# A's key weights on two DMA queues: rows 2, 4 and 6 issued by ScalarE, each after a one-column copy

## The chip, the cores and the metric

The kernel runs on one core of a Trainium2 chip. The time is the device time of one execution in microseconds; before the change the median of five runs is 474.25 us (474.18 to 474.83).

A core has TensorE (PE, matrix products), VectorE (DVE), ScalarE (ACT), GpSimd (POOL) and SyncE (SP). In a profile "PEld" is the loading of the stationary operand of a matmul, and "SPq" or "ACTq" is an engine at issuing a DMA.

## The reference, cut to what matters

Two attention blocks read the same `x` (2048 rows of 1024, bf16) and are mixed by a gate. Block A is linear attention; its keys are where the change lies.

```python
x = A_x
g = _sigmoid((x * gate_w).sum(-1, keepdims=True))
a = _A_ref(x, A_wqkv, A_wo)      # linear attention, 32 heads of 32
b = _B_ref(x, B_wqkv, B_wo)      # dilated sliding window, 8 keys
return g * a + (1 - g) * b

# in _A_ref
phi = lambda t: jnp.where(t > 0, t + 1, jnp.exp(t)) + 1e-6
pq, pk = phi(q), phi(k)          # q, k, v = x @ wqkv, split
kv = jnp.einsum("bhsd,bhse->bhde", pk, v)
z = jnp.einsum("bhsd->bhd", pk)
o = num / den                    # pq with kv, pq with z
return o ... @ wo
```

## The kernel before, in words

The contraction over the 1024 inputs is cut into KT = 8 pieces of 128 rows, numbered by `kt`; the 2048 tokens are cut into NB = 16 blocks of 128, numbered by `t`. The stages follow each other on TensorE: A's keys `pk` (line 167), the product of `x` with `pk` (line 218), A's key-value matrix (238), B's values and A's queries (293 and 329), B's keys, queries and attention (387, 444, 466), and the output (584).

The change lies in the loads that feed the first stage. `WkA` (128 x 8 x 1024) holds the key columns of `A_wqkv`; "row kt" of it is 128 partitions by 1024, 256 KB, loaded by `load_wk` (line 99) on the queue of the engine that is given to it. `xT` holds `x` transposed; `load_xT` (line 95) loads its columns `kt` for the first four blocks by a DMA transpose from SyncE, and line 112 the other twelve blocks, 128 tokens each with all eight `kt`. Behind them on SyncE come the rows of `x`, the gate's weights and further weights (lines 113 to 121).

The order on SyncE and ScalarE is written out by hand (`manual_schedule`), and so is the order on TensorE. ScalarE issues row 0, SyncE issues everything else: `xT` 0, row 1, `xT` 1, row 2, `xT` 2-3, row 3, row 4, `xT` 4-5, row 5, row 6, `xT` 6-7, row 7, and then line 112. DMAs share eight completion semaphores in rotation; one that takes up a semaphore again waits until the earlier transfer on it has landed.

TensorE first runs 37 products of ones (`warm_up`, line 173). Then it takes the first four blocks and both halves of the 1024 columns together, in eight PSUM banks, and goes through the contraction in groups, so that it can start with the first rows:

```python
for kts_ in ((0,), (1,), (2, 3), (4, 5), (6, 7)):
    for half in range(2):
        for t in range(4):
            for kt in kts_:
                project(first[4 * half + t], t, kt, half)
```

Thus 8 products use row 0, 8 use row 1, and then 16 in turns rows 2 and 3. When the last group is through, `phi` (lines 153 to 155, ScalarE and VectorE) turns each bank into `pk`; after that block after block follows. `ones` is a constant tile, there before the first instruction of the program's body. ScalarE's first instruction is the load of a function table (line 68); after its issue of row 0 its next work is the first exponential of line 153.

Of the kernel before, what the change touches and what calls it, by code (L numbers as in the profile page):

```python
# [39 lines left out]
def kernel(  # L40
# [11 lines left out]
    nc = tc.nc  # L52
# [6 lines left out]
    def rows(ap, s0, s1):  # L59
        return ap[s0 // 1024, s0 % 1024:(s1 - 1) % 1024 + 1, :]  # L60
# [3 lines left out]
    KT = D // P  # L64
# [12 lines left out]
    def load_w(name, src, col0, tag, only=(0, 1)):  # L77
        halves = []
        for h in only:
            w = wpool.tile([P, KT, 512], BF16, name=f"{name}{h}", tag=tag)  # L80
            c0 = col0 + h * 512
            nc.sync.dma_start(out=w[:], in_=src[:, c0:c0 + 512].rearrange("(kt p) n -> p kt n", p=P))
            halves.append(w)
        return halves
# [4 lines left out]
    def load_rows(eng, t0, t1):  # L89
        eng.dma_start(out=xrow[:, t0:t1, :], in_=rows(x, t0 * P, t1 * P).rearrange("(t p) d -> p t d", p=P))  # L90

    WkA = wide.tile([P, KT, D], BF16, name="WkA", tag="wa")

    def load_xT(kt, n, t0, t1):
        nc.sync.dma_start_transpose(out=xT[:, kt:kt + n, t0 * P:t1 * P],  # L95
                                    in_=rows(x, t0 * P, t1 * P)[:, kt * P:(kt + n) * P])

    def load_wk(eng, kt):
        eng.dma_start(out=WkA[:, kt, :], in_=A_wqkv[kt * P:(kt + 1) * P, D:2 * D])  # L99

    ones = nc.const_aps.tensor(1.0, [P, P], BF16)
    with tc.manual_schedule(engines={SP, mybir.EngineType.Activation}):
        load_wk(nc.scalar, 0)
        load_xT(0, 1, 0, 4)
        load_wk(nc.sync, 1)
        load_xT(1, 1, 0, 4)
        for kt in range(2, KT):
            load_wk(nc.sync, kt)
            if kt % 2 == 0:
                load_xT(kt, 2, 0, 4)  # L110
        for t in range(4, NB):
            nc.sync.dma_start_transpose(out=xT[:, :, t * P:(t + 1) * P], in_=rows(x, t * P, (t + 1) * P))
        for t in range(0, NB, 4):
            load_rows(nc.sync, t, t + 4)
        gw_row = consts.tile([P, D], BF16, name="gw_row")
        nc.sync.dma_start(out=gw_row[:], in_=gate_w.partition_broadcast(P))
        WvA = load_w("WvA", A_wqkv, 2 * D, "wb")
        WoA = load_w("WoA", A_wo, 0, "wo")
        WvB = load_w("WvB", B_wqkv, 2 * D, "wc")
# [37 lines left out]
    with tc.manual_schedule(engines={PE}):  # L157

        with ExitStack() as s1:
# [42 lines left out]
            for t in range(1, NB):  # L202
                side.append(lambda t=t: nc.vector.tensor_tensor(
                    out=zacc[:], in0=zacc[:] if t > 1 else pk[:, 0, :], in1=pk[:, t, :], op=ALU.add))
            side.append(lambda: nc.gpsimd.partition_all_reduce(zrow[:], zacc[:], P, bass_isa.ReduceOp.add))
            for t in range(NB):
                side.append(lambda t=t: nc.vector.tensor_tensor_reduce(
                    out=gjunk[:], in0=xrow[:, t, :], in1=gw_row[:], scale=1.0, scalar=0.0, op0=ALU.mult,
# [151 lines left out]
        with ExitStack() as s2:  # L360
# [158 lines left out]
            for c in range(KT):  # L519
                kts[c] = kpool.tile([P, 2, 1024], BF16, name="kt", tag="kt")  # L520
                for hh in range(2):
# [3 lines left out]
                    if 1 <= c <= 2:  # L525
                        t = 2 * (c - 1) + hh
                        nc.sync.dma_start_transpose(out=pqT[0][:, :, t * P:(t + 1) * P],
                                                    in_=pqd[t * P:(t + 1) * P, :])
# [114 lines left out]
```

The softmax here doesn't subtract the row's maximum and nothing guards it: scores larger than these inputs give would overflow.

## Time and profile before

| | |
|---|---|
| median of five runs | 474.25 us (474.18 to 474.83) |
| the profiled execution's own time | 474.25 us |
| its span, first to last instruction | 472.5 us |
| PE busy | 468.5 us (99%) |
| DVE, ACT, POOL busy | 277.3, 169.1, 15.3 us |
| DMA moved | 55.40 MB, 117 GB/s on the mean |
| granted TensorE clock | 1.000 |
| ScalarE, first exponential of line 153 | starts at 17.14 us, after 15.06 us idle |
| SyncE, line 112 | first issued at 11.50 us, twelve in 17.35 us |

The busy time of an engine is the sum of its instructions; matmuls overlap, so a busy PE may still be slower than its peak. The "chain of waits" follows the program back from its last instruction to whatever released each step. A line of the timeline gives the start, the length, the engine, the source line, the operation, and in brackets the idle time before it with what ended it. In a table of stretches each row gives the stretch, its length, then busy time and count for PE, PEld, DVE, ACT and POOL, the granted clock, the share of the DMA engines (above 1 where packets overlap) and GB/s.

### The profile page before, as it was taken

What the parts mean: (1) busy time and instruction counts of PE and PEld (TensorE: products, weight loads), DVE (VectorE), ACT (ScalarE), POOL (GpSimd) and SP (SyncE); (2) the same over time, 40 slices, a digit from 0 to 9 for tenths busy, and PEclk for the clock granted to TensorE, in tenths of its full rate; (3) what the DMA queues carried; (4) which work ended last, traced back from release to release, by engine and by line L of the source; (5) the groups of instructions that cost most, each with busy time, mean ns of one, the idle gap of its engine ahead of it and who ended that gap; (6) DMA issues with size and microseconds to landing.
All of it is one profiled execution on the core that took longest, in us unless ns stands there. A gap on an engine that the chain in (4) does not pass through costs nothing.

```text
span 472.5 us, 13171 instructions
## 1 busy us (share of the span) xinstructions
PE 468.5 (99%) x5765; PEld 246.3 (52%) x5765; DVE 277.3 (59%) x601; ACT 169.1 (36%) x272; POOL 15.3 (3%) x30
## 2 busy tenths in 40 slices
PE   9999999999999999999999999999999999999997
PEld 5444444445444444445666666666665444444444
DVE  0496689990329999999567676767660049800000
ACT  1343321102533333333555555555551134221122
POOL 3300000500000000000000000000000000000000
PEclk9999999999999999999999999999999999999999
DMA  8999960000644233627326626442563843221101
GB/s 199 225 255 371 348 227 0 0 1 0 203 129 120 95 139 130 156 95 246 108 55 102 112 52 94 100 95 50 92 151 79 177 123 78 69 54 45 34 33 46
DMA packets 96716, 55.40 MB, mean 117 GB/s; under 512 B 70162, under 2 KB 86546, under 8 KB 96658
## 3 DMA queue, kind: packets, MB, share of 16 engines
q1 hardware_dynamic: 91618, 50.10, 41.4%
q10 hardware_dynamic: 5040, 4.46, 2.9%
q8 instruction: 45, 0.74, 0.6%
q14 instruction: 13, 0.11, 0.1%
HBM read 26.10 MB, written 15.86 MB: 89 GB/s over the span
## 4 chain that ended last, share of the span: by engine, by line
PE 97%; SPq 1%; DMA 1%; issue 0%; ACT 0%
PE q_ps L387 27%; PE d_ps L584 12%; PE p_ps L293 12%; PE g_ps L218 12%; PE e_ps L584 12%; PE pk_ps L167 11%; PE p_ps L329 9%; PE po L466 2%; PE s2b L444 2%; DMA WkA<-in_A_wqkv_dram 1%; SPq L95 1%; PE kv_ps L238 0%; PE w_ps L281 0%; SPq L99 0%; ACT osb L589 0%
## 5 line engine op out<-in xcount | busy, mean ns | idle before, releaser
L387 PE MATMUL q_ps<-xT,WqB 64*64 64x512 bf16 x1024 | 68.3, 377 | 0.0
L387 PE MATMUL q_ps<-xT,WkB 64*64 64x512 bf16 x1024 | 67.9, 377 | 0.0
L154 DVE TENSOR_SCALAR e<-e 128x512 f32<-128x512 f32 x64 | 27.0, 422 | 64.5 <-ACT e L153 64.5
L293 PE MATMUL p_ps<-WvB,xT 128*128 128x512 bf16 x256 | 57.7, 379 | 0.0
L167 PE MATMUL pk_ps<-WkA,xT 128*128 128x512 bf16 x256 | 56.5, 383 | 0.3 <-DMA WkA<-in_A_wqkv_dram 0.3
L218 PE MATMUL g_ps<-pk,xrow 128*128 128x512 bf16 x256 | 55.4, 379 | 0.0
L449 ACT ACTIVATE PT<-s2b 128x928 bf16<-128x928 f32 (+4 forms) x40 | 34.2, 854 | 45.5 <-PE s2b L444 45.5
L451 DVE TENSOR_TENSOR PT<-PT,mask 128x928 bf16<-128x928 bf16 (+4 forms) x40 | 23.6, 590 | 38.1 <-ACT PT L449 38.1
L329 PE MATMUL p_ps<-WqA,xT 128*128 128x512 bf16 x192 | 43.4, 379 | 0.0
L584 PEld LDWEIGHTS <-pqT 128*128 128x128 bf16 x272 | 26.0, 98 | 29.8 <-issue 0.4
L167 PEld LDWEIGHTS <-xT 128*128 128x128 bf16 x256 | 25.2, 99 | 31.2 <-issue 1.9
L584 PEld LDWEIGHTS <-OBT 128*128 128x128 bf16 x272 | 26.0, 98 | 29.4
L218 PEld LDWEIGHTS <-xrow 128*128 128x128 bf16 x256 | 25.0, 98 | 30.2
L293 PEld LDWEIGHTS <-xT 128*128 128x128 bf16 x256 | 24.7, 98 | 30.2 <-issue 0.9
L387 PEld LDWEIGHTS <-WkB 64*64 64x64 bf16 x1024 | 31.7, 107 | 15.4 <-issue 0.4
L387 PEld LDWEIGHTS <-WqB 64*64 64x64 bf16 x1024 | 31.4, 106 | 15.4 <-issue 0.7
L153 ACT ACTIVATE e<-pk_ps 128x512 f32<-128x512 f32 x32 | 18.9, 597 | 41.2 <-PE pk_ps L167 37.0
L298 ACT CAST tmp<-p_ps 128x512 bf16<-128x512 f32 x32 | 18.8, 590 | 35.9 <-PE p_ps L293 29.4
L584 PE MATMUL d_ps<-WoA,pqT 128*128 128x512 bf16 (+1 forms) x136 | 30.9, 370 | 0.0
L584 PE MATMUL d_ps<-WoB,OBT 128*128 128x512 bf16 (+1 forms) x136 | 30.8, 370 | 0.0
L329 PEld LDWEIGHTS <-xT 128*128 128x128 bf16 x192 | 18.8, 98 | 22.6
L584 PE MATMUL e_ps<-WoA,pqT 128*128 128x512 bf16 (+2 forms) x136 | 30.0, 363 | 0.0
(61 smaller groups left out, 486.6 us busy)
## 6 DMA issues: line engine op xcount, KB each, us to landing
vd<-tmp SPq DMA_DIRECT2D x16, 264.0 KB
xrow<-in_A_x_dram SPq DMA_DIRECT2D x4, 1024.0 KB
out_dram<-osb ACTq DMA_DIRECT2D x31, 128.0 KB
pqd<-tmp SPq DMA_DIRECT2D x12, 256.0 KB
WvA<-in_A_wqkv_dram SPq DMA_DIRECT2D x2, 1024.0 KB
WoA<-in_A_wo_dram SPq DMA_DIRECT2D x2, 1024.0 KB
WvB<-in_B_wqkv_dram SPq DMA_DIRECT2D x2, 1024.0 KB
WqA<-in_A_wqkv_dram SPq DMA_DIRECT2D x1, 2048.0 KB
```

Of the source, the lines that this page charges most:

```text
L153: nc.scalar.activation(out=e[:], in_=pj[:], func=ACT.Exp)
L154: nc.vector.tensor_scalar(out=e[:], in0=e[:], scalar1=1.0, scalar2=1e-6, op0=ALU.min, op1=ALU.add)
L167: nc.tensor.matmul(pj[:], lhsT=xT[:, kt, t * P:(t + 1) * P], rhs=WkA[:, kt, half * 512:half * 512 + 512], start=(kt == 0), stop=(kt == KT ...
L218: nc.tensor.matmul(pj[:], lhsT=xrow[:, t, kt * P:(kt + 1) * P], rhs=pk[:, t, half * 512:(half + 1) * 512], start=(t == 0), stop=(t == NB - 1))
L293: nc.tensor.matmul(st["pj"][:], lhsT=xT[:, kt, t * P:(t + 1) * P], rhs=WvB[half][:, kt, :], start=(kt == 0), stop=(kt == KT - 1))
L298: nc.scalar.copy(out=v[:, half * 16:(half + 1) * 16, 0:Dh], in_=st["pj"][:].rearrange("p (h e) -> p h e", h=16))
L329: nc.tensor.matmul(st["pj"][:], lhsT=xT[:, kt, t * P:(t + 1) * P], rhs=WqA[:, kt, half * 512:half * 512 + 512], start=(kt == 0), stop=(kt ...
L387: nc.tensor.matmul(banks[o][64 * j:64 * j + 64, :], lhsT=lhsT(r, kt, j), rhs=rhs(r, kt), start=first and kt == 0, stop=kt == KT - 1, skip_ ...
L444: nc.tensor.matmul(s2b[64 * par:64 * par + 64, pair, :, o:o + w], lhsT=kts[c][r, par, k0:k0 + 64], rhs=qz[r, :, par, q0 % 512:q0 % 512 + w ...
L449: nc.scalar.activation(out=pt[:, :, 0:W_], in_=s2b[:].rearrange("p a b s -> p (a b) s")[:, :, 0:W_], func=ACT.Exp, scale=SCALE)
L451: nc.vector.tensor_tensor(out=pt[:, :, 0:W_], in0=pt[:, :, 0:W_], in1=mask[:, None, base:base + W_].broadcast_to([P, 4, W_]), op=ALU.mult)
L584: nc.tensor.matmul(st["ps"][:, 0:n], lhsT=lhsT, rhs=W[c0 // 512][:, c, c0 % 512:c0 % 512 + n], start=(side == 0 and c == 0), stop=(side == ...
```

## The change

Rows 2, 4 and 6 of `WkA` are issued by ScalarE in place of SyncE. Ahead of each stands a copy, on ScalarE, of one column into that very row: the DMA overwrites the column, so it has to wait for the copy. The copy for row 2 reads `ones`, that for row 4 reads row 0 of `WkA`, and that for row 6 reads row 2, so these two wait until the row that they read has landed. SyncE keeps rows 1, 3, 5 and 7 and all transposes: `xT` 0, row 1, `xT` 1, `xT` 2-3, row 3, `xT` 4-5, row 5, `xT` 6-7, row 7, then the twelve blocks (line 114 after the change).

```diff
         load_xT(0, 1, 0, 4)
         load_wk(nc.sync, 1)
         load_xT(1, 1, 0, 4)
-        for kt in range(2, KT):
-            load_wk(nc.sync, kt)
-            if kt % 2 == 0:
-                load_xT(kt, 2, 0, 4)
+        for kt in (2, 4, 6):
+            src = ones if kt == 2 else WkA[:, kt - 4 if kt == 4 else 2, :]
+            nc.scalar.copy(out=WkA[:, kt, 0:1], in_=src[:, 0:1])
+            load_wk(nc.scalar, kt)
+            load_xT(kt, 2, 0, 4)
+            load_wk(nc.sync, kt + 1)
```

## The prediction

> **What bounds the kernel now.** First the page: TensorE is busy in 468.5 of 472.5 us, and the chain of waits gives it 97%. What is not PE is 1% DMA for `WkA` and about 1% for SyncE's issues of lines 95 and 99.
>
> ```profile
> PE 468.5 (99%) x5765; PEld 246.3 (52%) x5765; DVE 277.3 (59%) x601; ACT 169.1 (36%) x272; POOL 15.3 (3%) x30
> PE 97%; SPq 1%; DMA 1%; issue 0%; ACT 0%
> L167 PE MATMUL pk_ps<-WkA,xT 128*128 128x512 bf16 x256 | 56.5, 383 | 0.3 <-DMA WkA<-in_A_wqkv_dram 0.3
> ```
>
> The reader is to see that line 167, the product with A's key weights, has only 0.3 us of idle time before it. A change in the loading order can win what PE loses at the start, and no more. So next the chain over the first 60 us, in order of time (start, us, what):
>
> ```profile
> 3.91 0.58 SPq L99
> 4.49 0.04 issue
> 4.53 1.29 SPq L95
> 5.82 0.04 issue
> 5.87 3.91 DMA WkA<-in_A_wqkv_dram
> 9.78 0.04 issue
> 9.82 50.23 PE pk_ps L167 x232
> ```
>
> The chain goes through SyncE's issues one after the other, to the row of `WkA` issued at 5.87 (row 3), which lands at 9.78; from 9.82 PE runs without a gap. Then the timeline of PE and of its weight loads around that point:
>
> ```profile
> 0.84 4.11 PE L173 MATMUL warm<-const-bfloat16-1.0 128*128 128x128 bf16 x37 [0.84 <-PEq L627]
> 4.74 4.80 PE L167 MATMUL pk_ps<-WkA,xT 128*128 128x512 bf16 x17
> 9.82 2.53 PE L167 MATMUL pk_ps<-WkA,xT 128*128 128x512 bf16 x11 [0.28 <-DMA WkA<-in_A_wqkv_dram]
> 4.63 0.25 PEld L167 LDWEIGHTS <-xT 128*128 128x128 bf16 x2
> 6.79 2.04 PEld L167 LDWEIGHTS <-xT 128*128 128x128 bf16 x10 [0.20 <-issue]
> 9.14 0.13 PEld L167 LDWEIGHTS <-xT 128*128 128x128 bf16 x2 [0.30 <-DMA xT<-in_A_x_dram]
> ```
>
> Two stalls: 0.30 us before the weight load of 9.14 (columns 2 and 3 of `xT`), then 0.28 us before the matmul of 9.82 (row 3). Together 0.58 us. The first product starts at 4.63 because the 37 warm-up matmuls end there: `xT` 0 has landed at 4.22 and row 0 at 3.76 by the trace's completion events, and the change touches neither. The spacing of weight loads is 0.43 us up to about 6.5 us and about 0.216 us after 6.79, so PE turns to full speed there.
>
> **What the Trainium skill says.** "DMA: Bandwidth & Descriptors", section "Issuing engines are not separate DMA queues": transfers of SP and ACT run on the same 16 DMA engines, and a second issuer saves only the sequencer's issue time. The trace does show issue times of 0.58 us (SP) and 0.39 us (ACT) for one row, but also DMA time that is not full (below), which a second ring could fill. The same page, section "Queues, rings and completion order": an engine goes round its rings by packets, so a row on ACT's ring shares time with SP's transposes; the trace has nothing of this, since ACT has one early row only. "TensorE: Matmul & The Clock Gate", Part 1: the window that releases the clock runs free, so the point of full speed moves between runs. One profile cannot confirm that; it has the point near 6.6 us.
>
> **The change part by part.** Sums are against the profiled execution: 474.25 us, span 472.5, 1.75 around it; it equals the median of the five runs.
>
> (1) SyncE loses the issues of rows 2, 4 and 6, three of 0.58 us, 1.7 us in all. Columns 2-3 of `xT` go out at 3.91 in place of 4.53, row 3 at 5.25 in place of 5.87, columns 4-5 at about 5.85 (6.96), row 5 at 7.2 (8.40), columns 6-7 at 7.8 (9.49), row 7 at 9.2 (10.88), the twelve transposes of line 112 from 9.8 (11.50). Each reuses one of eight completion semaphores: row 5 waits for row 1, columns 6-7 for row 0, row 7 for columns 2-3. The first two have landed long before (5.73, 3.76); the last landed at 9.10 in this trace, just ahead of SyncE's arrival. So at worst some tenths, with row 7 needed by PE only at 16.5 (below).
>
> (2) ScalarE gains three copies and three issues. The table load ends at 2.08. A 128x1 copy on ScalarE takes 0.16 us here (`seen`, line 399, from PSUM; the nearest row), an issue 0.39. Row 2: copy at 2.1, issue at 2.3 to 2.7, where SyncE had 3.91. Row 4: its copy reads row 0 (landed 3.76), its issue also waits for the semaphore of `xT` 0 (4.22), so 4.3 to 4.7 in place of 6.4. Row 6: its copy reads row 2; from issue to landing the present rows take 2.9 to 4.2 us, so it is issued between 5.5 and 7.0 in place of 8.93. Behind them on ScalarE stands the first exponential of line 153, at 17.14, after 15.06 us idle: six instructions of 1.7 us in all, and two waits that end by 7, cost nothing. That cover would be gone only if row 2 landed after 16.
>
> (3) The order of the bytes. All is moved as before, but row 4 (and part of row 6) now runs ahead of row 3. From the trace's packet records a row is 128 packets of 2 KB at 84 ns, over 16 engines 0.67 us; a 128x512 piece of `xT` is 512 packets of 256 B at 18 ns, 0.58 us. The DMA share by stretches of 1 us:
>
> ```profile
> 4.00:5.00 1.00, 1.00 (x10) 0.89 (x9) 0.00 (x0) 0.00 (x0) 0.00 (x0) 1.00 0.74 240
> 7.00:8.00 1.00, 1.00 (x6) 0.49 (x5) 0.00 (x0) 0.00 (x0) 0.00 (x0) 1.00 0.74 114
> 8.00:9.00 1.00, 1.00 (x7) 0.39 (x4) 0.00 (x0) 0.00 (x0) 0.00 (x0) 1.00 1.17 306
> 9.00:10.00 1.00, 0.72 (x4) 0.23 (x3) 0.00 (x0) 0.00 (x0) 0.56 (x2) 1.00 1.04 341
> ```
>
> The last two columns are the share and GB/s. 114 GB/s at 7 us against 306 and 341 later: the early transfers are slow (single packets of 0.4 to 1.2 us among them), not short of engines. From 3.5 us, when row 1 starts, to 9.0, when the last packet of row 3 starts, are 5.5 us. The work in it is row 1, `xT` 1, row 2, `xT` 2-3, row 3: 0.67 + 0.58 + 0.67 + 1.15 + 0.67 = 3.74 us. So 1.76 us are lost to slow packets, and two rings can hide them behind each other. After the change 0.67 (row 4) to 1.34 us (rows 4 and 6) are added ahead of row 3. If all lost time is filled, row 3's last packet goes at 3.5 + 3.74 + 0.67 = 7.9, or 8.6 with row 6; landing follows some 0.75 us later (9.78 for 9.0): 8.7 to 9.3. If none is filled, 9.78 + 0.67 to 9.78 + 1.34, so 10.4 to 11.1. With two thirds filled (1.17 us) and all of row 4 with half of row 6 in front (1.0): 9.6. I take that. The fill is a choice between two bounds, no row shows it.
>
> (4) What it is worth. Without a stall PE would reach row 3's first product at 9.82 - 0.58 = 9.24. A landing of 9.6 makes that product start at 9.64, 0.18 us sooner; a landing under 9.2 gives the full 0.58. All that follows stays behind PE: at 0.216 us each, the 15 products left of rows 2 and 3 end at 13.1, where rows 4 and 5 are wanted (they land at 10.75 and 12.46 now, and are issued earlier after the change); rows 6 and 7 at 16.5 (14.83 now); `xT` of block 4 at 20.0 (15.79 now). So nothing is late next, and the shift passes to the end undiminished. Row 1 and `xT` 1 are the one point to watch: wanted at 7.2 (the ninth product), landed at 5.73 and 6.31; sharing with row 2 costs at most 0.67 us, so 6.98, still in time. **Sum:** -0.58 to +1.3, taken as -0.2: 474.25 - 0.2 = about 474.0.
>
> **The rivals.** No change that can be measured means within 0.2%, 0.95 us.
> - *Forecast, a small shift* (81%): 473.4 to 475.1, row 3's landing between 8.7 and 10.6. For it: the idle time at stake is 0.58 us.
> - *The holds do not hold, and row 3 is crowded out* (12%, slower): rows 4 and 6 are released by row 0 and row 2, which land before PE is half way through row 1, so they take up to 1.34 us of the engines just as columns 2-3 and row 3 travel. It decides from a landing of 10.73 (9.78 + 0.95); at the full price 474.25 + 1.3 = 475.6. For it: share over 1 from 8 us on. Against it: 114 GB/s at 7 us, room to fill.
> - *All stalls vanish and PE runs ahead* (7%, faster): if in most executions the full clock comes at 4.6 rather than 6.6, PE would reach row 3 by 4.63 + 17 x 0.216 = 8.3 and now waits to 9.78; a landing of 8.7 would then give 1.1 us: 473.15. Against it: it needs the best landing and the early clock together.
> - *It does nothing*: the engines are shared, the fill just pays for row 4; 474.25, part of the first case.
>
> **How the numbers follow.** Likeliest 474.0. Downward the range takes the full stall with a little of the early clock, 473.4; upward a landing of 10.6, 475.1. Faster by over 0.2% (below 473.3) 0.07, slower (above 475.2) 0.12, between them 0.81.
>
> **What would show it.** Right: ACT issues of `WkA` near 2.3, 4.3 and 5.5 to 7; SyncE's line 114 (112 before) starting near 9.8; stalls before row 3's product under 0.6 us; no gap of PE later. Wrong: a wait of PE for `xT` 1 near 7 us, a wait for row 3 beyond 10.7, ACT held past 16, or any PE gap after 13 us that is not there now.

## The result and the profile after

| | before | after |
|---|---|---|
| median | 474.49 us (473.86 to 476.87, 48 runs) | 476.29 us (474.25 to 478.32, 27 runs) |
| profiled execution, its span | 474.25, 472.5 us | 476.77, 475.1 us |
| ratio after to before | | 1.0031, 95% interval 1.0022 to 1.0040 |

The change makes the kernel slower, by 0.3% or 1.8 us between the medians (1.0 to 1.9 us by the interval); the forecast was 474.0 us in a range of 473.4 to 475.1. A part of the runs of several of these kernels, the one before among them, has a mean TensorE clock of 0.996 in place of 1.000 and is some 2 us longer; where such runs are many (6 of 15 in e2, 8 of 22 in e13, below), the median of the others follows in brackets.

The page of the changed kernel, first PE's row, then the group of line 169 (167 before):

```profile
PE 467.4 (98%) x5765; PEld 244.5 (51%) x5765; DVE 277.3 (58%) x601; ACT 169.7 (36%) x275; POOL 15.4 (3%) x30
L169 PE MATMUL pk_ps<-WkA,xT 128*128 128x512 bf16 x256 | 55.9, 379 | 3.6 <-DMA xT<-in_A_x_dram 3.1
```

PE's idle time before products of this line was 0.3 us and is 3.6 us, and what ended most of it is now a transpose of `xT`, not a row of `WkA`. The chain of waits over the first 60 us (start, us, what):

```profile
3.89 1.30 SPq L95
5.19 0.04 issue
5.24 6.73 DMA WkA<-in_A_wqkv_dram
11.96 0.04 issue
12.01 48.07 PE pk_ps L169 x222
```

Row 3 is issued at 5.24 instead of 5.87, as the change wants, but takes 6.73 us to land instead of 3.91. The timeline of PE, then of the weight loads:

```profile
4.24 1.89 PE L169 MATMUL pk_ps<-WkA,xT 128*128 128x512 bf16 x8
8.38 1.90 PE L169 MATMUL pk_ps<-WkA,xT 128*128 128x512 bf16 x8 [2.25 <-DMA xT<-in_A_x_dram]
11.15 0.39 PE L169 MATMUL pk_ps<-WkA,xT 128*128 128x512 bf16 x1 [0.88 <-DMA xT<-in_A_x_dram]
12.01 10.30 PE L169 MATMUL pk_ps<-WkA,xT 128*128 128x512 bf16 x47 [0.47 <-DMA WkA<-in_A_wqkv_dram]
4.19 1.45 PEld L169 LDWEIGHTS <-xT 128*128 128x128 bf16 x8
```

Three stalls: 2.25 us for `xT` 1, 0.88 for `xT` 2-3, 0.47 for row 3. Row 3's first product starts at 12.01, before it was 9.82: 2.19 us later. A gap of 0.4 us on PE in the attention stage, which the trace of the kernel before doesn't have and for which no cause is known, makes 2.6 with it: the two spans differ by 475.1 - 472.5 = 2.6. The eight weight loads in 1.45 us also show PE at full speed from its first product here; before it was so only after 6.5 us.

ScalarE's timeline:

```profile
2.09 0.19 ACT L109 COPY WkA<-const-bfloat16-1.0 128x1 bf16<-128x1 bf16 x1
2.31 0.34 ACTq L99 DMA_DIRECT2D WkA<-in_A_wqkv_dram  x1
3.71 0.19 ACT L109 COPY WkA<-WkA 128x1 bf16<-128x1 bf16 x1 [1.42 <-DMA WkA<-in_A_wqkv_dram]
4.22 0.33 ACTq L99 DMA_DIRECT2D WkA<-in_A_wqkv_dram  x1
6.94 0.20 ACT L109 COPY WkA<-WkA 128x1 bf16<-128x1 bf16 x1 [3.04 <-DMA WkA<-in_A_wqkv_dram]
8.41 0.34 ACTq L99 DMA_DIRECT2D WkA<-in_A_wqkv_dram  x1
```

Row 4 goes out at 4.22, when `xT` 0 has landed. A ring, in what follows, is the queue of one issuing engine; a packet is one piece of a transfer in the trace's records, 2 KB of a row or 256 B of a transpose. The packets of row 4 start at 6.9 us, after the last of row 2 on ScalarE's ring, and end at 10.8, beside the transposes of columns 2-3 on SyncE's ring. Both are slow: a packet of row 4 takes 191 ns on the mean in place of 84, and the transposes pass 19 to 133 packets in each 0.25 us from 7.0 to 9.75. A transpose that travels alone at its best passes about 280 (282 and 284 in the kernel before from 12.75 to 13.25); but it can be slow alone too, as in the kernel before, where 19 to 58 passed in each 0.25 us from 7.0 to 7.75 with nothing on the other ring. So a slow stretch needs no second ring; the changed kernel's is longer. Its stretches (last two columns: DMA share and GB/s):

```profile
6.00:7.00 1.00, 0.13 (x1) 0.00 (x0) 0.00 (x0) 0.06 (x1) 0.00 (x0) 1.00 1.04 164
7.00:8.00 1.00, 0.00 (x0) 0.00 (x0) 0.00 (x0) 0.13 (x1) 0.00 (x0) 1.00 1.27 171
8.00:9.00 1.00, 0.62 (x3) 0.31 (x4) 0.00 (x0) 0.00 (x0) 0.00 (x0) 1.00 1.05 164
```

171 and 164 GB/s from 7 to 9 us where the kernel before had 114 and 306, with the engines no less occupied. From 6 to 7 us the kernel before had 233:

```profile
6.00:7.00 1.00, 1.00 (x4) 0.39 (x3) 0.00 (x0) 0.00 (x0) 0.00 (x0) 1.00 1.51 233
```

### The profile page after: what moved, and what is told of

The parts are those of the page before. It is cut to its first block, busy times and chain, and to the rows that moved or that the text cites. A ratio compares the mean times of both kernels' runs of the same rounds, so it can differ in the third digit from the quotient of the medians.

```text
span 475.1 us, 13179 instructions
## 1 busy us (share of the span) xinstructions
PE 467.4 (98%) x5765; PEld 244.5 (51%) x5765; DVE 277.3 (58%) x601; ACT 169.7 (36%) x275; POOL 15.4 (3%) x30
## 3 DMA queue, kind: packets, MB, share of 16 engines
q10 hardware_dynamic: 5472, 5.25, 3.7%
## 4 chain that ended last, share of the span: by engine, by line
PE 97%; DMA 1%; SPq 1%; issue 0%; ACT 0%
PE q_ps L389 26%; PE d_ps L586 12%; PE p_ps L295 12%; PE g_ps L220 12%; PE e_ps L586 11%; PE pk_ps L169 11%; PE p_ps L331 9%; PE po L468 2%; PE s2b L446 2%; DMA WkA<-in_A_wqkv_dram 1%; SPq L95 1%; PE kv_ps L240 0%; PE w_ps L283 0%; SPq L99 0%; ACT osb L591 0%
```

## The experiments

The theories: (1) rows 4 and 6 are released too early, and their bytes travel in front of columns 2-3 and row 3; (2) a row on ScalarE's ring slows the transposes beside it on SyncE's ring by more than its own engine time; (3) the order on SyncE's ring, two transposes one behind the other, is slow. Each median is to be set against that of the kernel before, run in the same session: 474.55 us for e1 to e4, 474.51 for e5 to e8, 474.37 for e9 to e12, 474.49 for e13 and e14. The diffs stand against the kernel before (e1 to e4, e11, e12) or the changed one (the rest); "hold(r, s)" is short for the copy of a column of s into row r and the issue of row r on ScalarE.

| | median, us | ratio (95%) | `xT` 1, `xT` 2-3 landed | row 3's first product |
|---|---|---|---|---|
| before | 474.49 | | 6.31, 9.10 | 9.82 |
| after | 476.29 | 1.0031 (1.0022 to 1.0040) | 8.33, 11.11 | 12.01 |
| e1 row 2 alone | 474.01 | 0.9984 (0.9974 to 0.9994) | 7.82, 8.92 | 9.8 |
| e2 row 4 alone | 475.08 (474.85) | 1.0023 (1.0010 to 1.0036) | 6.46, 9.89 | 10.61 |
| e3 row 6 alone | 474.51 | 1.0000 (0.9992 to 1.0009) | 6.48, 9.07 | 9.86 |
| e4 one ring | 474.17 | 0.9992 (0.9984 to 1.0000) | 6.82, 7.91 | 9.63 |
| e5 rows 2, 4 | 475.98 | 1.0024 (1.0013 to 1.0034) | 8.61, 12.02 | 12.6 |
| e6 no rows 4, 6 | 473.78 | 0.9984 (0.9977 to 0.9991) | 7.91, 8.88 | 9.9 |
| e7 later holds | 473.78 | 0.9981 (0.9972 to 0.9990) | 7.78, 8.83 | 9.8 |
| e8 row 4 ahead | 474.38 | 0.9997 (0.9989 to 1.0005) | 7.30, 8.99 | 9.76 |
| e9 row 2 held too | 474.43 | 1.0002 (0.9991 to 1.0013) | 6.42, 8.89 | 9.63 |
| e10 no copies | 473.82 | 0.9987 (0.9979 to 0.9996) | 7.43, 8.41 | 9.4 |
| e13 row 4 with ones | 475.36 (474.97) | 1.0031 (1.0017 to 1.0046) | 9.06, 9.81 | 11.1 |
| e14 row 0's bytes | 476.64 | 1.0043 (1.0033 to 1.0053) | 7.40, 10.15 | 10.81 |

The landings (a transfer's completion events) come from one trace each, so the medians decide and a trace only illustrates. The traces of e4, e8 and e14 are of runs among the fastest of their kernel, that of e5 of one among the slowest. A value with one decimal is counted on from the last restart of PE at 0.216 us a product, or read from the weight loads (e5).

**e1, row 2 alone**

```diff
-        for kt in range(2, KT): ...
+        hold(2, ones); load_xT(2, 2, 0, 4)
+        load_wk(nc.sync, 3); load_wk(nc.sync, 4); load_xT(4, 2, 0, 4)
+        load_wk(nc.sync, 5); load_wk(nc.sync, 6); load_xT(6, 2, 0, 4); load_wk(nc.sync, 7)
```

> Only row 2 goes to ScalarE, behind its copy of ones; rows 4 and 6 stay on SyncE in their old places. Theory 1 (bytes ahead: rows 4 and 6, released too early, travel in front of columns 2-3 and row 3): no loss, within 0.4 us of before, the columns of xT 1 land before 7.0 us. Theory 2 (any row on ScalarE's ring slows the transposes that travel beside it, beyond its own 0.67 us): slower by 0.7 to 1.5 us, PE waits for xT 1 near 7 us. Theory 3 (the order on SyncE's ring, two transposes next to each other, is what is slow): slower by 0.5 to 2 us.

0.5 us faster. But `xT` 1 landed at 7.82, not before 7.0, and 1.5 us later than before. How much of that comes from sharing with row 2 isn't shown: row 2's last packet ended at 6.2, and from 7.25 to 7.75 the transposes passed 2 and 20 packets in 0.25 us with nothing beside them. PE makes up for the wait, since all that follows is there:

```profile
7.87 12.47 PE L173 MATMUL pk_ps<-WkA,xT 128*128 128x512 bf16 x55 [1.47 <-DMA xT<-in_A_x_dram]
```

One wait, and no further one. Theory 2 forecast the late landing, but the time that it forecast with it did not come.

**e2, row 4 alone**

```diff
-            load_wk(nc.sync, kt)          # kt = 4
+            hold(4, row 0)                # in its place
```

> Only row 4 goes to ScalarE, behind its copy of row 0; rows 2 and 6 stay on SyncE. Theory 1: slower by 1 to 2 us, since row 4 is issued near 4.2 us and runs ahead of columns 2-3 and row 3; PE waits for those near 9 to 12 us, and not for xT 1. Theory 2: slower by 0.5 to 1.5 us, in the transposes of xT 1 or 2-3. Theory 3: no change, within 0.4 us.

0.5 us slower between the medians, 475.08 (474.85). Columns 2-3 are late, `xT` 1 is not: as theory 1 has it, but with about half of the least loss that it forecast. With no row 2 ahead of it on ScalarE's ring, row 4 ran from 5.2 to 8.0 us, mostly beside row 2 on the other ring. PE's wait for columns 2-3:

```profile
9.93 0.39 PE L173 MATMUL pk_ps<-WkA,xT 128*128 128x512 bf16 x1 [0.93 <-DMA xT<-in_A_x_dram]
```

**e3, row 6 alone**

```diff
-            load_wk(nc.sync, kt)          # kt = 6
+            hold(6, row 2)                # in its place
```

> Only row 6 goes to ScalarE, behind its copy of row 2; rows 2 and 4 stay on SyncE. Row 2 lands near 8 us, so row 6 is issued after that and its bytes come when row 3 has nearly landed. Theory 1: within 0.3 us of before. Theory 2: a loss only if the transposes of columns 4-5 slip past 13 us, so 0 to 0.5 us. Theory 3: no change.

No difference: row 6 was issued at 8.29, and its packets ran from 11.0 us on, after row 3 had landed (9.82).

**e4, one ring, transposes next to each other**

```diff
-        for kt in range(2, KT): ...
+        for kt in (2, 4, 6):
+            load_xT(kt, 2, 0, 4)
+            load_wk(nc.sync, kt); load_wk(nc.sync, kt + 1)
```

> Nothing goes to ScalarE but row 0; SyncE issues all in the order xT 1, xT 2-3, row 2, row 3, xT 4-5, row 4, row 5, xT 6-7, row 6, row 7, so that the transposes of xT 1 and 2-3 follow each other as in the changed kernel, on one ring. Theories 1 and 2: within 0.4 us of before. Theory 3: slower by 1.5 to 2.5 us, as the changed kernel.

474.17, at the edge of being faster. Theory 3 falls: this order alone brings columns 2-3 in at 7.91 in place of 9.10.

**e5, rows 2 and 4 on ScalarE**

```diff
-            hold(6, row 2)
+            load_wk(nc.sync, 6)
```

> Rows 2 and 4 go to ScalarE behind the copies of the change; row 6 stays on SyncE. The loss of the change is larger than that of row 4 alone. Theory 1a (row 4 on top of row 2 makes all of it, row 6 is innocent): 1.3 to 2.2 us slower than before, row 3's first product waits past 11 us, as in the changed kernel. Theory 1b (row 6 adds its part): at most the 1.1 us of row 4 alone.

475.98, 1.5 us over the kernel before: the slow kernel again, though row 6 is back in its old place, so no cost of row 6 shows. The stretches show the same hole, a microsecond longer:

```profile
7.00:8.00 1.00, 0.48 (x3) 0.00 (x0) 0.00 (x0) 0.00 (x0) 0.00 (x0) 1.00 1.19 130
8.00:9.00 1.00, 0.34 (x2) 0.21 (x3) 0.00 (x0) 0.00 (x0) 0.00 (x0) 1.00 1.09 123
9.00:10.00 1.00, 1.00 (x7) 0.43 (x5) 0.00 (x0) 0.00 (x0) 0.60 (x2) 1.00 1.22 155
```

**e6, rows 4 and 6 not loaded**

```diff
-            hold(4, row 0); hold(6, row 2)
-                 rhs=WkA[:, kt, half * 512:half * 512 + 512],
+                 rhs=WkA[:, {4: 0, 6: 2}.get(kt, kt), half * 512:half * 512 + 512],
```

> Rows 4 and 6 are not loaded at all; the products of rows 4 and 6 use rows 0 and 2 in their place, which leaves out two transfers of 256 KB and makes the values of A's keys others. The order on SyncE and row 2 on ScalarE are those of the changed kernel. Theory 1 (the bytes of row 4 in front): no loss, 473.4 to 474.2 us, like row 2 alone; PE waits only for xT 1. If a loss over 1 us stays, the short spacing of SyncE's issues is the cause and not the rows.

473.78 (one of its 22 runs took 491.24, with no cause known): the loss goes with the rows. The close spacing of SyncE's issues does no harm by itself.

**e7, later holds**

```diff
-            hold(4, row 0); hold(6, row 2)
+            hold(4, row 2); hold(6, row 3)
```

> The changed kernel with later holds: the copy for row 4 reads row 2 (landed near 7 us in the changed kernel) in place of row 0, that for row 6 reads row 3 in place of row 2. All six instructions on ScalarE and the order on SyncE stay. Theory 1 (the release of row 4 is too early): the loss is gone or under 0.7 us; row 3's product starts before 10.5 us. Theory 2 (traffic on ScalarE's ring beside transposes is slow whenever it comes): a loss of 1 us or more stays, moved to row 4's products near 13 us.

473.78, 0.7 us faster than before and some 2.5 faster than the changed kernel, with all six instructions on ScalarE in place. Row 4 is issued at 7.61 in place of 4.22. Its packets run from 9.8 to 10.5 us, behind columns 2-3, row 3 and columns 4-5 and ahead of row 5, so it shares the engines with almost nothing and takes its 0.7 us:

```profile
7.61 0.36 ACTq L99 DMA_DIRECT2D WkA<-in_A_wqkv_dram  x1
7.83 12.48 PE L175 MATMUL pk_ps<-WkA,xT 128*128 128x512 bf16 x57 [0.63 <-DMA xT<-in_A_x_dram]
8.00:9.00 1.00, 1.00 (x6) 0.47 (x5) 0.00 (x0) 0.00 (x0) 0.00 (x0) 1.00 1.07 294
```

(ScalarE's and PE's timeline, then a stretch.) One wait for `xT` 1 is left, and the rate at 8 us, when columns 2-3 end and row 3 travels, is 294 GB/s against 164. So the moment of row 4's release decides. Theory 2, that a row on ScalarE's ring is slow beside transposes whenever it comes, is not tested by this run, since row 4 met none.

**e8, row 4 ahead, on SyncE's ring**

```diff
-            hold(4, row 0); hold(6, row 2)
+        # SyncE: xT 1, row 4, xT 2-3, row 3, xT 4-5, row 5, row 6, xT 6-7, row 7
```

> Row 2 on ScalarE as in the change, but row 4 goes out on SyncE's ring, right behind xT 1 and ahead of columns 2-3 and row 3; row 6 on SyncE in its old place. So row 4's bytes are in front of row 3 as in the changed kernel, without a second ring at that moment. If only bytes count, row 3's product comes 0.67 to 0.85 us later than with row 2 alone and the time is 474.6 to 474.9 us. If sharing two rings is what costs, the same bytes cost clearly less than in the kernel with rows 2 and 4 on ScalarE. If it is as slow as that kernel (1.3 to 2.2 us over before), the ring doesn't matter.

474.38, no loss against before, with the same rows in front as e5 and only the ring of row 4 another. Here row 4's bytes are in front of columns 2-3 as in the changed kernel, but they take their turn, and then the transposes pass 282 packets in 0.25 us:

```profile
7.00:8.00 1.00, 1.00 (x6) 0.31 (x4) 0.00 (x0) 0.00 (x0) 0.00 (x0) 1.00 1.09 295
8.00:9.00 1.00, 1.00 (x6) 0.39 (x4) 0.00 (x0) 0.00 (x0) 0.20 (x1) 1.00 1.16 330
```

295 and 330 GB/s, where rows 2 and 4 on ScalarE (e5) had 130 and 123. By the medians the bytes in front cost 0.4 us against e1; on the other ring at this moment, about 2.0 (e5 to e1). So theory 1 holds for the moment, and theory 2 for the price at that moment.

**e9, row 2 held by row 0 as well**

```diff
-            hold(2, ones); hold(4, row 0); hold(6, row 2)
+            hold(2, row 0); hold(4, row 2); hold(6, row 3)
```

> As the kernel with later holds, and row 2 is held too: its copy reads row 0 (landed near 3.7 us) in place of the tile of ones. What is left in that kernel is a wait for xT 1 near 7.8 us, since row 2 travels beside row 1 and xT 1. If that sharing causes it, xT 1 lands under 7.2 us, its wait is gone, and the time is 473.3 to 473.7 us. If row 2 then runs beside columns 2-3 instead and slows those as row 4 did in the changed kernel, row 3's product starts after 10 us and the time is 474.3 us or more.

474.43, the second of the two outcomes, or near it: `xT` 1 landed at 6.42 and its wait is nearly gone, but row 2 now travels partly beside columns 2-3, which land at 8.89, and PE waits for those. The gain of e7 is spent. The runs fall into two groups, nine from 473.70 to 474.56 and five from 475.28 to 475.60, and the trace is of one of the first; what the second waited for isn't known.

**e10, no copies**

```diff
-            nc.scalar.copy(out=WkA[:, kt, 0:1], in_=src[:, 0:1])
```

> Rows 2, 4 and 6 on ScalarE without the copies; only the rotation of the eight completion semaphores holds row 6 (until row 1 has landed). Row 4 is then issued before 2.5 us in place of 4.2. Theory 1 (row 4 beside columns 2-3 does the harm): the bytes of rows 2 and 4 now run beside row 1 and xT 1, and row 6 beside columns 2-3, so a loss of 1.5 to 3 us stays, the wait for xT 1 grows past 8.5 us. If the copies do nothing at all: the same as the changed kernel, 476.0 to 476.6 us.

473.82. My expectation was wrong here, the loss is gone. Rows 2 and 4 are issued right behind row 0. The packets of row 2 run from 3.3 to 4.3 us and those of row 4 from 4.2 to 6.1, 95 of its 128 begun before 5.0, so mostly ahead of row 1:

```profile
3.00:4.00 1.00, 1.00 (x13) 1.00 (x11) 0.00 (x0) 0.00 (x0) 0.00 (x0) 1.00 1.18 335
4.00:5.00 1.00, 0.94 (x9) 0.68 (x7) 0.00 (x0) 0.00 (x0) 0.00 (x0) 1.00 1.01 285
7.47 12.69 PE L172 MATMUL pk_ps<-WkA,xT 128*128 128x512 bf16 x58 [0.33 <-DMA xT<-in_A_x_dram]
```

335 and 285 GB/s against 169 and 180 in the changed kernel. `xT` 0 lands 0.9 us later (5.12), and PE starts its first product 0.4 us later, but `xT` 1, which from about 6 us has the engines to itself, lands at 7.43. So in the changed kernel the holds moved row 4 out of a place where it did no harm and into the worst of those tried.

**e11 and e12, the sharing of the rings measured by itself**

```diff
             nc.sync.dma_start_transpose(out=xT[:, :, t * P:(t + 1) * P], ...)
+            if t == 7:          # e11; in e12 nc.sync issues it, without the copy
+                nc.scalar.copy(out=WvA[0][:, 0, 0:1], in_=xT[:, 0, 4 * P:4 * P + 1])
+                nc.scalar.dma_start(out=WvA[0][:], in_=wsrc[0])
```

> The kernel before, with one later load moved: 1 MB of A's value weights goes out on ScalarE, held by a copy out of block 4 of xT until about 16 us, so that it runs beside SyncE's transposes of blocks 6 to 15, where nothing on TensorE waits. If sharing two rings is slow in itself, these transposes crawl and the rate falls under 200 GB/s over some microseconds; the last block lands clearly later than with the same load on SyncE. If only the first microseconds of a kernel are like that, the rate stays at 200 to 300 GB/s.

> The same load at the same place in the order, but on SyncE's ring, between the transposes of blocks 7 and 8: the reference for the run with it on ScalarE. The transposes keep their pace of about 1.2 us a block and the load takes 3 to 4 us of its own.

One execution each (473.84 and 474.78 us, too few to compare), with nothing on PE that waits. Block 7 landed at 24.57 with the load on ScalarE and at 20.70 with it on SyncE, the load itself at 24.25 and 24.62, block 15 at 35.76 and 35.07. From 20 to 24 us both moved about the same, 1057 and 1197 KB. So the rings together lose little, 12% of the rate there; but the division of the bytes is far from even: beside the load the transposes passed 12 to 75 packets in each 0.25 us from 20 to 22 us, about a quarter of their pace or less. The Trainium skill, "DMA: Bandwidth & Descriptors", section "Queues, rings and completion order", says that an engine goes round its rings by packets. If the trace's packets are those that it means, e11 agrees: from 21.0 to 22.25 us the transposes passed 313 packets of 256 B and the load 312 of 1 KB. The changed kernel does not: from 7.0 to 9.75 us 745 packets of columns 2-3 stand against 113 of row 4, which is 191 KB against 231. Turns by packets can't explain its loss either, since by them the transposes would lose the row's own time at most, some 0.7 us at full pace, where columns 2-3 landed 2.0 us later; what is lost beyond that is lost by both rings together.

**e13, row 4's copy reads the tile of ones**

```diff
-            hold(4, row 0)
+            hold(4, ones)
```

> The changed kernel with one thing other: the copy for row 4 reads the tile of ones, as that for row 2 does, in place of row 0. Row 4 is then issued near 2.9 us in place of 4.2; all three copies, and row 6's hold on row 2, stay. If the moment of row 4's release makes the loss, and the copies themselves cost nothing: row 4 travels beside row 1 and xT 1, ahead of columns 2-3, and the time is 473.7 to 474.5 us, as without copies. If the copies or row 6's hold make the loss: 475.5 us or more, as in the changed kernel.

475.36 (474.97): between the two outcomes. Row 4 was issued at 2.92, but stood behind row 2 and ran from 6.1 to 8.2 us, now beside `xT` 1, which landed at 9.06. The harm moved from columns 2-3 to `xT` 1, which can wait longer before it costs, as rows 2 and 3 follow at once:

```profile
9.11 11.18 PE L175 MATMUL pk_ps<-WkA,xT 128*128 128x512 bf16 x50 [1.73 <-DMA xT<-in_A_x_dram]
```

The copies are not what costs time: e7 has three as well, and gains.

**e14, row 4's transfer reads bytes already read**

```diff
-            load_wk(nc.scalar, 4)
+            nc.scalar.dma_start(out=WkA[:, 4, :], in_=A_wqkv[0:P, D:2 * D])
```

> The changed kernel, with row 4's transfer at its place, moment and size, but reading the bytes of row 0 again (read once before, some 2 us earlier), so that A's keys come out other. If the slow first packets of a part of the weights never read before (0.2 to 0.8 us each in row 4) are what holds up the transposes beside them: the loss shrinks to under 1 us. If the sharing of the engines by two rings alone does it: still 1.3 us or more over before, with a wait for columns 2-3 past 10.5 us.

476.64, as slow as the changed kernel. Slow first reads of row 4's bytes are not the cause. The profiled execution is the fastest of this kernel's runs (475.02), so its landings understate the loss.

## Why the prediction was wrong, point by point

- **What bounds the kernel: right.** The start of row 3's first product is carried to the end: in all 14 traces of the table, the span less that start is 462.3 to 463.1 us. The limit of the gain was about right: e7 and e10 gain 0.7 and 0.55 us on the medians, where 0.58 was at stake. The two idle times that make the 0.58 are of two engines and shouldn't be added; by the starts of the weight loads, row 3's first would have come at 6.79 + 11 x 0.216 = 9.17 without a stall, 0.65 before 9.82. The traces of e1, e6 and e7 have row 3 start as late as before (9.8 to 9.9), so they don't show where these three gain.
- **SyncE's issues: right to row 5, then wrong.** Row 3 at 5.24 (5.25 forecast), columns 4-5 at 5.86, row 5 at 7.31. The issue of columns 6-7 then took 3.78 us in place of 1.34, and row 7 went out at 11.94 (9.2 forecast). Line 114 starts at 12.57, later than the 11.50 of before: the 1.7 us saved on SyncE are gone. This costs nothing further: PE waits for no transfer after 12.01.

```profile
8.12 3.78 SPq L95 DMA_TRANSPOSE xT<-in_A_x_dram  x1
```

- **ScalarE's six instructions: right in price** (a copy 0.19 us, an issue 0.34), rows 2 and 4 right in time. Row 6 went out at 8.41, not between 5.5 and 7.0: I had left out that its DMA takes up the semaphore of `xT` 1, which landed at 8.33.
- **The step that failed is part (3), the order of the bytes,** with the sentence on row 1 and `xT` 1 in part (4). It priced a row on the second ring at its engine time at full pace, 0.67 us, taken from whatever it displaces, less what it hides. `xT` 1 was given 6.98 at the latest and landed at 8.33; row 3 was given 11.1 at the worst and landed at 11.96. What the runs showed in its place: row 4, released onto ScalarE's ring at 4.22, lasted not 0.67 but 3.9 us (6.9 to 10.8), and columns 2-3 beside it landed 2.0 us later than before (11.11 for 9.10). In e5 it is the same, 4.6 us and 12.02. In e8, with row 4 ahead of columns 2-3 on the one ring, row 4 lasts 1.4 us and columns 2-3 land at 8.99.
- **"Two thirds of the lost time are filled": wrong.** From 6 to 9 us the changed kernel moved 164 + 171 + 164 = 499 KB, the one before 233 + 114 + 306 = 653. With two rings the lost time was not filled, more was lost. Why the rate sinks so far here, and by only 12% between e11 and e12, stays open. Both rings carry slow packets in this stretch, the kernel before has a slow stretch of 0.75 us on one ring, and e14 excludes that the newness of row 4's bytes makes the loss. The depth of the hole also varies: e5's runs spread from 474.67 to 476.89.
- **The slower rival named the mechanism, but not its size.** It had rows 4 and 6 released too early, and 475.6 at the full price. Row 4 it was, of row 6 no cost shows (e3, e5), and the time was 476.3. The argument against it, room to fill at 7 us, took a low rate for room that a second ring can use.
- **The early clock:** PE ran at full speed from its first product in the profile after, at 6.5 us in that before. The Trainium skill, "TensorE: Matmul & The Clock Gate", Part 1, has the point move between runs, and these two traces, with the same warm-up, agree. It makes the wait for `xT` 1 longer but not the landing of row 3 later.

## What to carry to other kernels

A second DMA queue does not only save issue time: a transfer on it competes at once with whatever the first queue carries. Here the same row ahead of the same transposes cost 0.4 us on their own queue (e8 to e1) and about 2.0 on the other (e5 to e1). So release a transfer on the second queue before or after the transposes that are wanted next, and look up in the trace when each transfer's packets run, not when it is issued: row 4's began 2.2 us after the issue in e7 and 2.65 in the changed kernel. A hold is only as good as the moment that it picks: here three copies lose 1.8 us with row 4 behind row 0, and win 0.7 with it behind row 2, while no hold at all wins 0.55.

## What the runs showed of the hardware that was not expected

- Beside a plain load on the other ring, DMA transposes passed 12 to 133 packets in 0.25 us in place of about 280 (after from 7.0 to 9.75 us, e11 from 20 to 22), while the two rings together moved between 0.76 (after against before, 6 to 9 us) and 0.88 (e11 against e12, 20 to 24 us) of what one ring did.
- Transposes can be as slow with nothing beside them: 19 to 58 packets in 0.25 us in the kernel before from 7.0 to 7.75 us. No run here shows what makes these stretches.
- In e11, from 21.0 to 22.25 us, two rings with packets of 256 B and 1 KB passed 313 and 312 of them, so one for one.
- With rows 2 and 4 issued on ScalarE at 1.24 and 1.72 us (e10), the core moved 335 and 285 GB/s from 3 to 5 us; with them issued at 2.31 and 4.22 (after), 169 and 180.
